# Pooled attention and MLP on one core: a product placed behind the scores, and queries loaded, pooled and bounded in earlier steps

## The chip, the cores and the metric

The kernel runs on one core of a Trainium2 chip. Its engines are TensorE (PE; PEld is its weight load), VectorE (DVE), ScalarE (ACT), GpSimd (POOL) and SyncE (SP), whose queue issues nearly all transfers. The metric is the time of one execution on the device in microseconds (us); less is better.

## The reference, cut to what matters

```python
# q, k, v: (4, 8, 1152, 64); out: (4, 576, 512)
q_pool = q.reshape(B, H, S // 2, 2, D).mean(axis=3)
scores = 1 / sqrt(D) * q_pool @ k.transpose(0, 1, 3, 2)
attn = exp(scores - max(scores)); attn = attn / (sum(attn) + 1e-9)
x = (attn @ v), heads side by side            # (4, 576, 512)
xn = (x - mean(x)) / sqrt(var(x) + 1e-6) * g_ln
out = x + relu(xn @ w_ch1) @ w_ch2            # w_ch1: 512 x 2048, w_ch2: 2048 x 512
```

All of it is in float32.

## The kernel before, in words

**Steps.** Two heads of one batch make a pair; there are 16 pairs (0 to 15), 4 to a batch. A pair is worked off in 9 steps of 128 query rows against 1152 keys (the fifth step takes 64 rows of either head), 144 steps in all. `step(i)` writes the instructions of step i in a fixed order, and each engine works through its own instructions in that order. `on_pe(i)` is true for the first batch, steps 0 to 35. In the list below a pair's steps are counted from its first, and "third step" has index 2.

**What a step does.** TensorE computes the scores of step i+1 (`emit_s`, L365 and L373) into one of two slots of three PSUM banks, by the parity of the step. VectorE takes the row maximum (L384), ScalarE the exponential into a `pe` tile (L398); there are two `pe` buffers, so the exponential of step i overwrites the one of step i-2. In the first batch TensorE transposes the probabilities in float32 (L431), and a product with the values follows (`emit_pv`, L455), its evacuation (L971) and a transposition back (`emit_turn`, L483). From step 36 on the probabilities are split into two float16 parts, the high one by ScalarE (L412), the low one by VectorE (L421) or, in the third, sixth and ninth step of a pair, by GpSimd (L254, then L419; `low_on_pool`). A DMA on the SP queue transposes both (L424), and four steps on the product runs on TensorE (L467). Once a batch is complete, its MLP is spread over later steps in units (L619, L651). These, and transpositions, share PSUM banks 6 and 7, which come free when ScalarE (L632, L289, L580) and VectorE (L633, L286, L581) have read them.

**Queries.** Four loads (`load_q`, L131) bring the queries of an even pair p and of the pair after it, into one of two `qr` buffers. They are pooled by one addition (`pool_q`, L166), then copied to stand twice (`dup_q`, L172), and ScalarE sums their absolute values for the bound on their size (`bound`, L188), which the scale needs (`scales_reduce`, whose VectorE part is L235 to L249). With the scale known, TensorE transposes them (L328) and ScalarE and VectorE split them (L289, L286). Keys (L115) and values (L119) have loads of their own for each pair.

**What sets the order.** Two tables: `pre(i, ...)` puts work ahead of step i's, `at(i, ...)` behind it; and `calm`, a list from which each step takes one piece, in order, mostly of splitting the weights (`w_split_a`, `w_split_b`, `w_split_c`, GpSimd). A loop over the pairs fills the tables; there `i0 = (p - 1) * C` with C = 9 is the first step of the pair before p. For p = 8, 10, 12 and 14 queries are loaded at i0-8, pooled ahead of i0-5 (the fifth step of pair p-2), bounded at i0-3 and copied at i0-1.

Of the kernel before, what the change touches and what calls it, by code (L numbers as in the profile page):

```python
# [14 lines left out]
ALU = mybir.AluOpType  # L15
# [9 lines left out]
def tile_pooled_attention_moe(  # L25
# [18 lines left out]
    nc = tc.nc  # L44
# [110 lines left out]
    def qt_of(p):  # L155
# [2 lines left out]
            st["qt"] = tr_p.tile([128, 2, 2 * C * 64], FP16, tag="qt", name="qt")  # L158
        return st["qt"]

    def pool_q(p, eng, halves=None):

        a = raws[p, "q"]
        for o, n in ((0, 128),) if halves is None else halves:
            x = a[o:o + n].rearrange("p h c r d -> p (h c) r d")
            eng.tensor_tensor(x[:, :, 0], x[:, :, 0], x[:, :, 1], op=ALU.add)  # L166

    def dup_q(p, eng, halves=None):
        a = raws[p, "q"]
        for o, n in ((0, 128),) if halves is None else halves:  # L170
            x = a[o:o + n].rearrange("p h c r d -> p (h c) r d")
            eng.tensor_copy(x[:, :, 1], x[:, :, 0])  # L172

    def bound(p, which, o=0, n=128, junk=None):
        st = state(p)
        if which == "q":
            src = raws[p, "q"][o:o + n].rearrange("p h c r d -> p (h c) r d")[:, :, 0]
            if on_pe((p - 1) * C) or p == 0:
                junk = qt_of(p)[o:o + n, 0].rearrange("p (a d) -> p a d", d=D)
            else:  # L180
                junk = raws[p, "q"][o:o + n].rearrange("p h c r d -> p (h c) r d")[:, :, 1]
        else:
            src = raws[p, which][o:o + n, :, 0:C].rearrange("p a b d -> p a (b d)")
            if junk is None:
                junk = kt_of(p)[o:o + n].rearrange("p a h n -> p (a h n)")[:, 0:S]
                junk = junk.rearrange("p (a n) -> p a n", a=2)
        m = "kqv".index(which)
        nc.scalar.activation(out=junk, in_=src, func=ACTF.Abs, accum_out=st["acc"][o:o + n, m:m + 1])  # L188
# [150 lines left out]
    def on_pe(i):  # L339

        return 0 <= i < HP * C
# [135 lines left out]
    def emit_turn(n, ot, i):  # L477

        j = n % C
        ps = psum[:, 3 * (i % 2) + 2, 128:258]  # L480
        parts = [(h, 64 * h, 64) for h in range(2)] if j == 4 else [(0, 0, 128)]
        for h, q0, w in parts:
            nc.tensor.transpose(ps[0:w, 65 * h:65 * h + 65], ot[:, q0:q0 + w], ident[0:65, 0:65])  # L483
        one, two = evac_pv(n, ps)
        found.extend((one, two, lambda: evacuated(n)))
# [308 lines left out]

    def w_split_c(n):
        x = wsl[:, n + 1].rearrange("p a n -> p (a n)").bitcast(FP32)
        nc.gpsimd.tensor_tensor(wsl[:, n, 1], x, wsl[:, n, 0], op=ALU.subtract)
        w_done[n // 4] += 1


# [2 lines left out]
    def at(i, fn, *a):  # L803
        todo.setdefault(i, []).append((fn, a))
# [10 lines left out]
    for p in range(1, NP):  # L815
# [2 lines left out]
        at(i0, load, p, "v", nc.sync)  # L818
        at(i0 + 1, bound, p, "k")
        if p % 2 == 0:  # L820
            if on_pe(i0):
                at(i0 - 4, load_q, p, (nc.sync,))
                at(i0 - 1, lambda p=p: calm.appendleft((lambda n: pool_q(p, nc.gpsimd), 0)))
                at(i0, lambda p=p: calm.appendleft((lambda n: dup_q(p, nc.gpsimd), 0)))
            else:
                x = i0 - (6 if p == 6 else 5)
                at(i0 - 8, load_q, p, (nc.sync,))
                pre(x, pool_q, p, nc.gpsimd)
                at(i0 - 1, dup_q, p, nc.gpsimd)
            at(i0 + 2 if on_pe(i0) else x + 2, bound, p, "q")  # L830
        elif p == 1:
            upper = (64, 64)
            pre(0, behind_scales)
# [146 lines left out]
    def step(i):  # L980
# [8 lines left out]
            steps.pop(i - 1)  # L989
        while found:  # L990
            found.popleft()()
        first = on_pe(i - 2) or on_pe(i)
        final, last[:] = list(last), []
        if first and not on_pe(i):
            a_piece(i)
# [150 lines left out]
```

## Time and profile before

| | |
|---|---|
| time, median of 3 runs | 839.42 us (837.78 to 840.08) |
| the profiled execution's own time | 839.62 us |
| its span, first to last instruction | 837.8 us |
| TensorE busy | 809.8 us, 97% |
| VectorE busy | 606.2 us, 72% |
| ScalarE busy | 558.4 us, 67% |
| GpSimd busy | 351.8 us, 42% |
| mean granted TensorE clock | 0.993 of full speed |
| moved by DMA | 115.97 MB, mean 138 GB/s |

The span is of one execution, which lies 1.8 us below that execution's time. Busy time is a union of an engine's instructions; TensorE's ends are modelled, so its share reads high.

### The profile page before, as it was taken

To read this page: it belongs to the slowest core of one execution; us is meant where nothing else is said; L and a number is where in the kernel's file an instruction comes from. 1 tells how busy PE (TensorE), PEld (TensorE's weight loads), DVE (VectorE), ACT (ScalarE), POOL (GpSimd) and SP (SyncE) were. 2 spreads that over 40 slices of the span, in tenths; PEclk is the share of its full clock that TensorE was granted. 3 is DMA by queue.
4 is the path that set the end of the run, shared out by engine and by line. 5 is a ranking of instruction groups with operands and counts; after the bars stand their busy time and mean duration, and the time that the engine had idled before them with its cause. 6 is when DMAs were issued, how large, how long until landed. Compare 5 with 4: busy or idle time off the path is not lost.

```text
span 837.8 us, 21673 instructions
## 1 busy us (share of the span) xinstructions
PE 809.8 (97%) x9142; PEld 576.7 (69%) x9142; DVE 606.2 (72%) x1167; ACT 558.4 (67%) x810; POOL 351.8 (42%) x343
## 2 busy tenths in 40 slices
PE   7999999987999989999999999999999999999997
PEld 6787878776666666757576766766666767767764
DVE  3598989887888878797887878888787877522221
ACT  3999898976777868787776777677867676311110
POOL 3020334286899982456452553636343432200000
PEclk9999999999999999999999999999999999999999
DMA  6944474125698998899989988996969866401001
GB/s 146 256 164 156 141 210 163 43 60 113 115 181 141 194 172 191 153 185 185 167 147 166 212 167 144 176 196 113 204 125 194 137 126 131 95 2 26 14 1 25
DMA packets 276018, 115.97 MB, mean 138 GB/s; under 512 B 259280, under 2 KB 259280, under 8 KB 275920
## 3 DMA queue, kind: packets, MB, share of 16 engines
q1 hardware_dynamic: 275568, 113.70, 66.0%
q8 instruction: 71, 1.16, 0.6%
q10 hardware_dynamic: 352, 0.88, 0.5%
q14 instruction: 27, 0.22, 0.1%
HBM read 46.14 MB, written 4.72 MB: 61 GB/s over the span
## 4 chain that ended last, share of the span: by engine, by line
PE 70%; DVE 12%; ACT 9%; DMA 4%; issue 3%; POOL 1%; SPq 1%; ACTq 0%; DVEq 0%; POOLq 0%
PE psum L619 21%; PE psum L651 20%; PE psum L467 10%; PE psum L365 8%; ACT pe L398 3%; DVE mx L384 3%; PE psum L373 2%; PE psum L455 2%; DMA kr<-in_k_dram 2%; PE psum L328 2%; PE psum L431 1%; DVE hl L421 1%; ACT pt L437 1%; PE psum L300 1%; DMA stage<-in_moe_w_ch_dram 1%
## 5 line engine op out<-in xcount | busy, mean ns | idle before, releaser
L384 DVE TENSOR_REDUCE mx<-psum 128x1 f32<-128x1152 f32 x144 | 194.3, 1349 | 21.3 <-PE psum L204 6.9
L398 ACT ACTIVATE pe<-psum,nb,sc 128x1152 f32<-128x1152 f32 x144 | 188.6, 1310 | 13.8 <-DVE r L516 5.7
L651 PE MATMUL psum<-wsl,ht 128*128 128x512 f16 x864 | 196.7, 379 | 0.0
L619 PEld LDWEIGHTS <-wsl 128*128 128x128 f16 x1920 | 170.1, 98 | 22.8 <-issue 4.0
L619 PE MATMUL psum<-xn,wsl 128*128 128x256 f16 x1536 | 177.9, 274 | 3.6 <-DVE ht L633 2.8
L651 PEld LDWEIGHTS <-ht 128*128 128x128 f16 x864 | 80.5, 98 | 88.0
L632 ACT ACTIVATE ht<-psum 128x512 f16<-128x512 f32 x72 | 42.9, 596 | 135.4 <-PE psum L619 134.1
L365 PE MATMUL psum<-kt,qt 64*128 64x512 f16 (+1 forms) x960 | 127.4, 380 | 0.7 <-ACT pe L398 0.5
L412 ACT ACTIVATE hl<-pe 128x1152 f16<-128x1152 f32 x108 | 125.6, 1163 | 3.4
L467 PE MATMUL psum<-vt,pt 128*128 128x65 f16 (+1 forms) x3240 | 117.0, 193 | 0.3 <-DMA pt<-hl 0.3
L467 PEld LDWEIGHTS <-pt 128*128 128x128 f16 (+1 forms) x3240 | 108.5, 100 | 3.1 <-DMA pt<-hl 0.4
L421 DVE SCALAR_TENSOR_TENSOR hl<-pe,hl 128x1152 f16<-128x1152 f32 x72 | 109.4, 1519 | 0.0
L633 DVE SCALAR_TENSOR_TENSOR ht<-psum,ht 128x512 f16<-128x512 f32 x72 | 49.6, 689 | 71.6 <-ACT ht L632 71.6
L254 POOL TENSOR_SCALAR pe<-pe 128x1152 f32<-128x1152 f32 x36 | 42.4, 1178 | 140.5 <-ACT hl L412 140.5
L419 POOL TENSOR_TENSOR hl<-pe,hl 128x1152 f16<-128x1152 f32 x36 | 85.5, 2376 | 3.0
L455 PE MATMUL psum<-pt,vt 128*65 128x128 f32 (+1 forms) x720 | 78.9, 265 | 1.9 <-DVE qt L286 1.9
L455 PEld LDWEIGHTS psum<-pt,vt 128*65 128x65 f32 x720 | 73.1, 140 | 2.2 <-DVE qt L286 2.2
L365 PEld LDWEIGHTS <-qt 64*128 64x128 f16 (+1 forms) x960 | 39.6, 96 | 38.7 <-issue 22.1
L373 PEld LDWEIGHTS <-qt 128*128 128x128 f16 (+1 forms) x320 | 17.2, 99 | 62.9 <-issue 62.7
L286 DVE SCALAR_TENSOR_TENSOR qt<-psum,s,qt 128x384 f16<-128x384 f32 x48 | 29.5, 615 | 34.6 <-ACT qt L289 34.3
L260 POOL COPY gate<-gate 128x1 f32<-128x1 f32 x27 | 5.2, 194 | 110.9 <-DVE gate L259 110.9
L665 DVE SCALAR_TENSOR_TENSOR xb<-psum,inv,xb 128x512 f32<-128x512 f32 x32 | 23.8, 745 | 36.9 <-PE psum L651 36.9
(117 smaller groups left out, 1028.4 us busy)
## 6 DMA issues: line engine op xcount, KB each, us to landing
stage<-in_moe_w_ch_dram SPq DMA_DIRECT2D x32, 512.0 KB, 6.0
kr<-in_k_dram SPq DMA_DIRECT2D x16, 576.0 KB, 4.4
qr<-in_q_dram SPq DMA_DIRECT2D x31, 288.0 KB, 6.2
vr<-in_v_dram SPq DMA_DIRECT2D x15, 576.0 KB, 4.8
out_dram<-xb SPq DMA_DIRECT2D x32, 128.0 KB, 2.4
pt<-hl SPq DMA_TRANSPOSE x108, 4.7
kr<-in_k_dram SPq DMA_DIRECT2D x16, 64.0 KB, 4.1
vr<-in_v_dram ACTq DMA_DIRECT2D x1, 576.0 KB, 7.2
```

Source lines behind the costliest of these rows:

```text
L365: nc.tensor.matmul(out=sp[o:o + w, c0:c0 + 512], lhsT=qt[r:r + 64, qa, q0:q0 + w], rhs=kt[r:r + 64, ka, h], start=(a == 0), stop=(a == 2),)
L384: nc.vector.tensor_reduce(mx, st["s"], axis=AX.X, op=ALU.max)
L398: nc.scalar.activation(out=st["pe"], in_=st["s"], func=ACTF.Exp, scale=pair[i // C]["sc"][:, 0:1], bias=st["nb"],)
L412: nc.scalar.activation(out=hl[:, 0], in_=st["pe"], func=ACTF.Copy, scale=2.0 ** 15)
L419: nc.gpsimd.tensor_tensor(hl[:, 1], st["pe"], hl[:, 0], op=ALU.subtract)
L421: nc.vector.scalar_tensor_tensor(hl[:, 1], st["pe"], 2.0 ** 15, hl[:, 0], op0=ALU.mult, op1=ALU.subtract)
L455: nc.tensor.matmul(out=ps[0:65, q0:q0 + w], lhsT=vt[:, h, c], rhs=pt[:, 128 * u + q0:128 * u + q0 + w], start=(u == 0), stop=(u == C - 1),)
L467: nc.tensor.matmul(out=dst[:, 0:n], lhsT=lhsT, rhs=rhs, start=(u == 0 and lhsT is hi and n == 65), stop=(u == C - 1 and lhsT is lo), skip_ ...
L619: nc.tensor.matmul(out=ps[:, o:o + n], lhsT=wsl[:, 8 * w + cc, wa, f * 128:f * 128 + 128], rhs=xn[:, xa * KD + cc, 0:n], start=(m == 0), s ...
L632: lambda: nc.scalar.activation(out=hi, in_=pv, func=ACTF.Relu),
L633: lambda: nc.vector.scalar_tensor_tensor(lo, pv, 0.0, hi, op0=ALU.max, op1=ALU.subtract),
L651: nc.tensor.matmul(out=ps, lhsT=hv[0][:, ha, f, t * 128:t * 128 + 128], rhs=wsl[:, 8 * w + 4 + f // 2, wa, (f % 2) * DM:(f % 2) * DM + DM] ...
```

## The change

The product of step 34 (`first` in `step`) is written behind the next scores in place of ahead of them, and `emit_turn` takes the other slot's bank from step 36 on. Queries of pairs 4 and 5 are loaded and pooled six steps earlier than they were, copied four and bounded seven. For p = 8, 10, 12, 14 the loads go from i0-8 to i0-9, the pooling from i0-5 to i0-7 (the third step of pair p-2) and the bound from i0-3 to i0-6; for p = 6 the load goes to i0-9, the pooling stays at i0-6, and the bound goes one step ahead. From step 36 on a pooling, a copy and a `w_split_c` is written as two instructions of half the length (`cuts`).

```diff
+    def cuts(x):
+        return (x,) if on_pe(this[0]) else (x[:, 0:C], x[:, C:2 * C])
+
     def pool_q(p, eng, halves=None):
...
-            eng.tensor_tensor(x[:, :, 0], x[:, :, 0], x[:, :, 1], op=ALU.add)
+            for y in cuts(x):
+                eng.tensor_tensor(y[:, :, 0], y[:, :, 0], y[:, :, 1], op=ALU.add)
 
     def dup_q(p, eng, halves=None):
...
-            eng.tensor_copy(x[:, :, 1], x[:, :, 0])
+            for y in cuts(x):
+                eng.tensor_copy(y[:, :, 1], y[:, :, 0])
 
     def bound(p, which, o=0, n=128, junk=None):
...
-            if on_pe((p - 1) * C) or p == 0:
+            if p < 4:
                 junk = qt_of(p)[o:o + n, 0].rearrange("p (a d) -> p a d", d=D)
...
     def emit_turn(n, ot, i):
 
         j = n % C
-        ps = psum[:, 3 * (i % 2) + 2, 128:258]
+        ps = psum[:, 3 * ((i if on_pe(i) else pv_slot[0]) % 2) + 2, 128:258]
...
     def w_split_c(n):
         x = wsl[:, n + 1].rearrange("p a n -> p (a n)").bitcast(FP32)
-        nc.gpsimd.tensor_tensor(wsl[:, n, 1], x, wsl[:, n, 0], op=ALU.subtract)
+        for y in (slice(0, 1024),) if on_pe(this[0]) else (slice(0, 512), slice(512, 1024)):
+            nc.gpsimd.tensor_tensor(wsl[:, n, 1, y], x[:, y], wsl[:, n, 0, y], op=ALU.subtract)
         w_done[n // 4] += 1
...
         if p % 2 == 0:
-            if on_pe(i0):
+            if p == 4:
+                at(i0 - 10, load_q, p, (nc.sync,))
+                at(i0 - 7, lambda p=p: calm.appendleft((lambda n: pool_q(p, nc.gpsimd), 0)))
+                at(i0 - 4, lambda p=p: calm.appendleft((lambda n: dup_q(p, nc.gpsimd), 0)))
+            elif on_pe(i0):
                 at(i0 - 4, load_q, p, (nc.sync,))
                 at(i0 - 1, lambda p=p: calm.appendleft((lambda n: pool_q(p, nc.gpsimd), 0)))
                 at(i0, lambda p=p: calm.appendleft((lambda n: dup_q(p, nc.gpsimd), 0)))
             else:
-                x = i0 - (6 if p == 6 else 5)
-                at(i0 - 8, load_q, p, (nc.sync,))
+                x = i0 - (6 if p == 6 else 7)
+                at(i0 - 9, load_q, p, (nc.sync,))
                 pre(x, pool_q, p, nc.gpsimd)
                 at(i0 - 1, dup_q, p, nc.gpsimd)
-            at(i0 + 2 if on_pe(i0) else x + 2, bound, p, "q")
+            if on_pe(i0):
+                x = i0 + 1 if p == 2 else i0 - 6
+            at(x + 1, bound, p, "q")
...
-        first = on_pe(i - 2) or on_pe(i)
+        first = on_pe(i - 1) or on_pe(i)
```

**On TensorE, steps 37 and 38.** The rows below are of the kernel before: L328 transposes queries, L574 a normalised tile, L455 is the product of step 34, L365 the scores of step 38, L483 the transposition back, L215 spreads a weight bound to all partitions.

```order
L328 MATMUL psum<-ident,qr 128x64 x6
L574 MATMUL psum<-ident,xs 128x128 x4
L455 MATMUL psum<-pt,vt 65x128 x9
L365 LDWEIGHTS qt
L365 MATMUL psum<-kt,qt 128x512
...
L483 MATMUL psum<-ident,pt 128x65
L215 MATMUL psum<-dg,ones_85 128x1
```

The same place in the changed kernel, whose lines are numbered 5 higher there.

```order
L333 MATMUL psum<-ident,qr 128x64 x6
L579 MATMUL psum<-ident,xs 128x128 x4
L370 LDWEIGHTS qt
L370 MATMUL psum<-kt,qt 128x512
...
L460 MATMUL psum<-pt,vt 65x128 x9
L220 MATMUL psum<-dg,ones_85 128x1
```

The product has moved behind the scores of step 38, and the transposition back, which needs it, behind those of step 39.

**On GpSimd, for pair 10 (steps 73 to 76).** Before: L191 copies a bound, L254 and L419 make the low half of the third step's probabilities, L562 to L568 normalise a tile, L166 pools.

```order
L191 COPY acc<-acc 128x1
L254 TENSOR_SCALAR pe<-pe 128x1152
L419 TENSOR_TENSOR hl<-pe,hl 128x1152
L562 TENSOR_SCALAR rs<-mv 128x1
L565 TENSOR_SCALAR rs<-mv 128x1
L566 TENSOR_TENSOR rs<-rs,nhalf 128x1
L568 TENSOR_SCALAR xs<-xb,rs 128x512
L166 TENSOR_TENSOR qr<-qr 128x18x64
```

In the changed kernel.

```order
L196 COPY acc<-acc 128x1
L170 TENSOR_TENSOR qr<-qr 128x9x64 x2
L259 TENSOR_SCALAR pe<-pe 128x1152
L424 TENSOR_TENSOR hl<-pe,hl 128x1152
L567 TENSOR_SCALAR rs<-mv 128x1
L570 TENSOR_SCALAR rs<-mv 128x1
L571 TENSOR_TENSOR rs<-rs,nhalf 128x1
L573 TENSOR_SCALAR xs<-xb,rs 128x512
```

The pooling, now in two halves, stands ahead of the low half and of the normalisation. For pair 8 a piece of splitting (L797, two halves) and a scaling (L254) of weights come between the pooling and the low half; before, the pooling stood behind all of them.

**On the SP queue, for pair 10 (steps 71 to 73).** Before: keys (L115, L116), a transposition of probabilities (L424), values (L119), a transposition, queries (L131).

```order
L115 DMA kr<-in_k_dram 128x2x576
L116 DMA kr<-in_k_dram 128x2x64
L424 DMA_TRANSPOSE pt<-hl 128x18x128
L119 DMA vr<-in_v_dram 128x2x576
L424 DMA_TRANSPOSE pt<-hl 128x18x128
L131 DMA qr<-in_q_dram 64x1152 x4
L670 DMA out_dram<-xb 64x512 x2
```

In the changed kernel.

```order
L115 DMA kr<-in_k_dram 128x2x576
L116 DMA kr<-in_k_dram 128x2x64
L429 DMA_TRANSPOSE pt<-hl 128x18x128
L119 DMA vr<-in_v_dram 128x2x576
L131 DMA qr<-in_q_dram 64x1152 x4
L429 DMA_TRANSPOSE pt<-hl 128x18x128
L675 DMA out_dram<-xb 64x512 x2
```

The four query loads have moved past one transposition, to directly behind the values.

## Rows read from the trace of the kernel before

**Rows 1.** The page: busy us (share of the span) and instructions by engine.

```profile
PE 809.8 (97%) x9142; PEld 576.7 (69%) x9142; DVE 606.2 (72%) x1167; ACT 558.4 (67%) x810; POOL 351.8 (42%) x343
```

**Rows 2.** Timeline, TensorE at the batch boundary: start, us, instructions [idle before <-releaser].

```profile
191.16 3.70 PE L455 MATMUL psum<-pt,vt 128*65 128x128 f32 x18 [1.94 <-DVE qt L286]
```

**Rows 3.** Windows: stretch, us, busy us by engine (instructions), PEclk, DMA share, GB/s.

```profile
190.91:194.32 3.41, 3.16 (x15) 3.16 (x16) 3.26 (x5) 0.00 (x0) 1.28 (x2) 0.50 0.02 5
```

**Rows 4.** Timeline, VectorE at the batch boundary.

```profile
194.02 0.18 DVE L557 BATCH_NORM_AGGREGATE mv<-bs 128x2 f32<-128x6 f32 x1
197.14 1.36 DVE L384 TENSOR_REDUCE mx<-psum 128x1 f32<-128x1152 f32 x1 [2.94 <-PE psum L215]
```

**Rows 5.** Timeline, SP queue: values ahead of pairs 8 to 14's queries; pair 10's.

```profile
285.01 0.58 SPq L119 DMA_DIRECT2D vr<-in_v_dram  x1
...
370.84 0.58 SPq L119 DMA_DIRECT2D vr<-in_v_dram  x1
...
375.83 2.50 SPq L131 DMA_DIRECT2D qr<-in_q_dram  x4
...
457.88 0.58 SPq L119 DMA_DIRECT2D vr<-in_v_dram  x1
...
546.07 0.58 SPq L119 DMA_DIRECT2D vr<-in_v_dram  x1
```

**Rows 6.** By source: landing of all L119; L131 of pair 10, ns, and its landing.

```profile
DMA to landing us min/median/max: 4.4/4.8/7.2
...
L131 SPq DMA_DIRECT2D qr<-in_q_dram x4: 589/592/596, 375.8 to 377.7; - x4
...
DMA to landing us min/median/max: 4.1/5.7/6.7
```

**Rows 7.** Timeline, GpSimd, steps 75 to 77.

```profile
375.92 1.16 POOL L254 TENSOR_SCALAR pe<-pe 128x1152 f32<-128x1152 f32 x1 [6.82 <-ACT hl L412]
377.16 2.38 POOL L419 TENSOR_TENSOR hl<-pe,hl 128x1152 f16<-128x1152 f32 x1
...
384.58 2.62 POOL L166 TENSOR_TENSOR qr<-qr 128x1152 f32<-128x1152 f32 x1 [3.10 <-DMA qr<-in_q_dram]
```

**Rows 8.** By source, L188: bounds of queries in the first batch, ns min/median/max, first and last.

```profile
L188 ACT ACTIVATE qt<-qr x4: 1154/1158/1164, 8.7 to 152.1; 64x1152 f16<-64x1152 f32 x2, 128x1152 f16<-128x1152 f32 x2
```

**Rows 9.** Timeline, TensorE, step 79.

```profile
396.82 0.63 PE L574 MATMUL psum<-ident,xs 128*128 128x128 f32 x4 [0.77 <-DVE qt L286]
```

**Rows 10.** Timeline, GpSimd: a scaling and a split of weights, steps 55 to 59.

```profile
282.25 1.12 POOL L254 TENSOR_SCALAR wsl<-wsl,wscl 128x1024 f32<-128x1024 f32 x1
...
300.56 2.12 POOL L797 TENSOR_TENSOR wsl<-wsl 128x1024 f16<-128x1024 f32 x1
```

**Rows 11.** Timeline, ScalarE: the exponentials of steps 58, 76, 94 and 112.

```profile
295.08 1.31 ACT L398 ACTIVATE pe<-psum,nb,sc 128x1152 f32<-128x1152 f32 x1
...
380.75 1.31 ACT L398 ACTIVATE pe<-psum,nb,sc 128x1152 f32<-128x1152 f32 x1
...
471.23 1.31 ACT L398 ACTIVATE pe<-psum,nb,sc 128x1152 f32<-128x1152 f32 x1
...
559.66 1.31 ACT L398 ACTIVATE pe<-psum,nb,sc 128x1152 f32<-128x1152 f32 x1
```

**Rows 12.** Timeline, VectorE: step 77's evacuation; step 112's low half.

```profile
384.20 0.75 DVE L286 SCALAR_TENSOR_TENSOR kt<-psum,s,kt 128x512 f16<-128x512 f32 x1 [0.43 <-ACT kt L289]
...
560.41 3.60 DVE L421 SCALAR_TENSOR_TENSOR hl<-pe,hl 128x1152 f16<-128x1152 f32 x1
```

**Rows 13.** Timeline, TensorE: pieces behind the exponentials of rows 11.

```profile
303.74 4.34 PE L619 MATMUL psum<-xn,wsl 128*128 128x256 f16 x24 [2.14 <-DVE ht L633]
...
385.36 0.60 PE L574 MATMUL psum<-ident,xs 128*128 128x128 f32 x4
...
477.59 2.75 PE L651 MATMUL psum<-wsl,ht 128*128 128x512 f16 x12
...
566.26 0.63 PE L574 MATMUL psum<-ident,xs 128*128 128x128 f32 x4 [1.77 <-DVE kt L286]
```

## The prediction

> **What bounds the kernel now.** I read the page first, then TensorE's and VectorE's timeline around the batch boundary, then for each even pair the SP queue, GpSimd, ScalarE and TensorE in the stretch where the change puts the pooling. TensorE is busy for 97% of the span [rows 1]. It works in program order, so whatever makes it wait is added to the time, and little is made up for later. At the batch boundary it waits 1.94 us in front of a product (L455), which then takes 3.70 us [rows 2], because the granted clock is 0.50, that is 1.2 GHz, from 190.91 to 194.32 [rows 3]. VectorE meanwhile is through at 194.20 and waits 2.94 us for the next scores [rows 4].
>
> The reader should see a second thing: queries arrive late. For pair 10 the SP queue issues the values at 370.84 and the four query loads from 375.83 [rows 5]; the first load lands 4.1 us after its issue, at 379.9, and the last, issued at 377.7, 6.7 us after, at 384.4 [rows 6]. Three of the four thus take 4.5 us, 1.5 each, and all four about 6.0 us of the DMA engines. GpSimd, now pooling in the fifth step, still waits 3.10 us for them and starts at 384.58 [rows 7].
>
> **The change, part by part.**
>
> *The product behind the scores, its transposition in the other slot.* TensorE has the scores ready to run when the last query transpositions are through, in the gap in which it now waits. The next row maximum can start when VectorE is free, at 194.20 in place of 197.14 [rows 4]: I take -2.9 us, since from there on the same chain follows. Bounds: 0, if the product, still in front of the following scores, holds these up as much; and -3.6, the wait of 1.94 and the 1.7 us that the half clock takes from 3.41 us [rows 2, 3].
>
> *Pair 4's queries earlier, the bound by seven steps.* Its bound leaves ScalarE's queue in step 29 and goes to step 22: 1.16 us [rows 8]. It can be worth all of it where it leaves and cost all of it where it goes, so I take -0.5 between +1.2 and -1.2. GpSimd does the same pieces in another order, and the four loads go out ahead of stage loads in place of among them; both have some steps to spare before anyone reads them: nothing.
>
> *Bounds of the later pairs three steps earlier.* For pair 10 this activation stands in front of the last query evacuations, and TensorE then waits 0.77 us on one [rows 9]: -0.8 (bounds 0 and -0.8; the other pairs show no wait there).
>
> *Pooling in the third step.* Here the DMAs decide. The loads move one step ahead, to directly behind the values, and so in front of one transposition; the pooling moves two steps ahead. The values land 4.8 us (median) after issue [rows 6]; the queries follow them in the queue and need 6.0 us more, so they land 10.8 us after the values' issue. The issues are 285.01, 370.84, 457.88 and 546.07 [rows 5], so they land at 295.8, 381.6, 468.7 and 556.9 for pairs 8, 10, 12 and 14: only about 2.8 us earlier than now for pair 10, while GpSimd comes to them about 9 us earlier. The first half waits for two loads and can begin before the last lands; of a 2.62 us pooling [rows 7] I let 1.6 follow the last landing: 297.4, 383.2, 470.3, 558.5.
>
> GpSimd's queue is in order, and behind the pooling now stands the low half of the third step's probabilities: L254 and L419, 3.6 us from 375.92 to 379.54 [rows 7]. For pair 8 a split in two halves (2.2 us, one whole is 2.12) and a scaling (1.1) [rows 10] stand between. L419 then ends at 304.3, 386.8, 473.9 and 562.1. Who waits: the exponential two steps on, since there are two `pe` buffers. It starts now at 295.08, 380.75, 471.23 and 559.66 [rows 11], so it comes 9.2, 6.1, 2.7 and 2.4 us late.
>
> Behind it ScalarE's queue holds the copy, the output and the evacuation that gives a PSUM bank back. For pair 10 that is 380.75 to the end of VectorE's L286 at 384.95, 4.2 us [rows 11, 12]; where L632 and L633 end it, about 4.0. TensorE's next piece, with two banks, starts at 308.3, 391.0, 477.9 and 566.3 against 303.74, 385.36, 477.59 and 566.26 [rows 13]: +4.6, +5.6, +0.3, 0. In pairs 8 and 14 the present waits (2.14 and 1.77) are thereby paid for and replaced, in pair 8 with the slow clock (4.34 us) as it is. Pair 10 gets a wait over 2 us that it lacks now; one more stretch of 3.41 us at half clock costs 1.7, and I take 1.6. Sum: +12.1. Cutting an instruction in two costs GpSimd a start each, under 0.1 us by the 2.2 above; in these stretches it waits for data longer than that: nothing.
>
> Rate against page: the row says 1.5 us for a load of 0.29 MB, some 197 GB/s. The Trainium skill, SBUF — State Buffer, section "A bandwidth-pool intuition that's wrong", gives HBM to a core about 358 GB/s. An estimate by that page is 3.3 us for all four loads, and a sum near 838; this case's rows don't show such a rate for queries.
>
> *Pair 6* loads one step earlier and pools where it did; its wait was hidden behind the boundary: nothing.
>
> **The sum**, against the profiled execution's 839.6 us: 839.6 - 2.9 - 0.5 - 0.8 + 12.1 = 847.5. The median shown is 839.4, 0.2 below, so 847.3.
>
> **Rivals.**
>
> *The loads are there in time (faster).* If the queries landed before GpSimd has its third-step work, 2.6 us before 375.92 in pair 10, i.e. by 373.3, the pooling would lie in idle time (6.82 us before that instruction [rows 7]), and its halves would hold VectorE less: L421 takes 3.60 us beside the whole pooling in pair 14 [rows 12]. Pair 8 would give back 2.14 + 1.7 and pair 14 1.77: 839.4 - 4.2 - 5.6 = 829.6. On why VectorE is held: the Trainium skill, SBUF — State Buffer, section "Who interferes with whom", has VectorE and GpSimd take a shared port pair for a whole instruction, which this row agrees with. Against this rival: even at the quickest landing, 4.1 us after the last issue, pair 10's queries come at some 377.5. I give 0.17, with what lies between.
>
> *Half as late (no change).* With that quickest landing in all pairs, some 6.6 us behind the values' issue, the poolings end at 293.2, 379.0, 466.1 and 554.3. By the same chain pairs 8 and 10 lose 0.4 and 1.4, pair 12 nothing, and pair 14 gains 1.8: about 835.2, the lower end. At some 8 us behind the issue, a third of the way from that to my 10.8, the four pairs cost a third of 12.1, some 4 us, which is what the earlier parts give: 839.4. For it speaks that the next transposition no longer stands ahead; against it, the engines' 1.5 us for each load. 0.12.
>
> *The boundary gives nothing and the clock falls oftener (much slower).* The loads 0.6 later (6.7 - 4.1 lies over the pure transfer, and the transposition displaced behind them lands late too, so its product waits in step four), 2.4 us; two more slow stretches, 3.2; no gain at the boundary, 2.9: some 856. For it speaks that TensorE's waits in pairs 8 and 10 come in two pieces each; against it, that these waits overlap. 0.16.
>
> *The forecast*, 842 to 852: 0.55.
>
> **How the numbers follow.** A measurement of this kernel tells about 0.3% from no change, 2.5 us. The forecast and the last rival are slower, 0.71; no change 0.12; faster 0.17. The predicted time is the likeliest case, 847. The range reaches down to the quickest landing, 835, and up to 856, leaving out most of the first rival and a little above; the forecast's own is 842 to 852.
>
> **What would show it.** In the changed kernel's trace: before the first half of L166 (now L170) GpSimd waits several us for the query loads in pairs 8 to 14, longest in pair 10; the exponential two steps on waits for GpSimd's L419 by some 9, 6, 2 and 2 us; TensorE has waits there and a granted clock of 0.50 after them. At the boundary VectorE's 2.94 us are gone and there is no slow stretch at 191. Wrong would be a query landing under 8 us after the values' issue, or an exponential that doesn't wait though L419 is late. If the pooling's waits are there and the time isn't longer, TensorE had other room than I saw.

## The result and the profile after

The changed kernel takes **846.12 us** (median of 6 runs, 843.87 to 848.66) against 838.84 (median of 6 runs, 837.52 to 842.41) beside it: a ratio of 1.0076, 95% interval 1.0052 to 1.0100. It is slower by some 7 us. The prediction was 847.0, between 835 and 856, with 0.71 on slower. The size is right. The way to it is right only in part, as the experiments show.

The profiled execution has a span of 845.0 us. First the page of the changed kernel: the engines (answering to [rows 1]), then two of its costliest groups, whose last column is the engine's idle time before them and what ended most of it.

```profile
PE 812.2 (96%) x9142; PEld 577.9 (68%) x9142; DVE 602.8 (71%) x1167; ACT 558.1 (66%) x810; POOL 360.4 (43%) x363
...
L403 ACT ACTIVATE pe<-psum,nb,sc 128x1152 f32<-128x1152 f32 x144 | 188.5, 1309 | 30.9 <-POOL hl L424 18.4
...
L472 PE MATMUL psum<-vt,pt 128*128 128x65 f16 (+1 forms) x3240 | 118.4, 194 | 8.3 <-DMA pt<-hl 8.3
```

TensorE, VectorE and ScalarE have the same instructions as before; GpSimd has 20 more, since some are halved, and is busy 8.6 us longer. What is new is waiting: ScalarE's exponential for GpSimd's low half (L424), 18.4 us in all (3.0 before), its bound for GpSimd's pooling, 9.4 us (none before), and TensorE's product (L472) for a transposition of probabilities by DMA, 8.3 us (0.3 before). The last was only a side remark in one of my rivals.

**Where the time went, step by step.** A step is taken to begin with its row maximum on VectorE (L384 before, L389 after). The table gives how much later that row starts than before, in one profiled execution of each, counted from step 20, up to which the kernels run alike (the starts of step 20 lie within 1.9 us of before's). Pair 4's edit acts up to step 31, the boundary up to 47, and pairs 8, 10, 12 and 14 in the stretches that end at steps 72, 90, 108 and 126. Behind 126 nothing differs.

| us later than before, at step | 31 | 40 | 47 | 56 | 72 | 90 | 108 | 126 |
|---|---|---|---|---|---|---|---|---|
| the change | -1.8 | -8.0 | -6.1 | -6.0 | -1.1 | +3.6 | +4.1 | +7.5 |
| loads four steps earlier | -1.8 | -8.0 | -6.1 | -5.6 | -8.6 | -7.7 | -7.6 | -9.8 |
| pooling back in the fifth step | -1.8 | -8.0 | -6.1 | -5.6 | -8.2 | -8.5 | -8.5 | -9.7 |
| loads of the third step, pooling in the fifth | -1.8 | -7.9 | -6.1 | -5.5 | -2.9 | +1.1 | +1.2 | +0.5 |
| low half on VectorE, bound later | -1.8 | -8.0 | -6.1 | -5.9 | -3.8 | +1.7 | +2.3 | +1.5 |
| loads behind the transposition | -1.8 | -8.0 | -6.1 | -6.0 | +4.3 | +12.2 | +17.8 | +22.6 |
| pooling in the third step alone | 0.0 | 0.0 | -0.1 | -0.1 | +4.6 | +9.6 | +11.3 | +15.7 |
| boundary alone | 0.0 | -5.4 | -0.3 | -0.2 | -2.4 | -1.2 | -1.2 | -1.2 |
| boundary and pair 6's lead | 0.0 | -5.5 | -4.1 | -4.1 | -2.3 | -2.6 | -2.6 | -1.2 |

So the change gains 6 us by step 56 and loses 4.9, 4.7, 0.5 and 3.4 us in pairs 8, 10, 12 and 14.

At the boundary, TensorE's and then VectorE's timeline of the changed kernel answer to [rows 2, 4], and the first window below to [rows 3].

```profile
187.87 2.18 PE L460 MATMUL psum<-pt,vt 128*65 128x128 f32 x18 [0.97 <-DVE qt L291]
...
191.63 2.13 PE L460 MATMUL psum<-pt,vt 128*65 128x128 f32 x18
```

```profile
190.65 0.18 DVE L562 BATCH_NORM_AGGREGATE mv<-bs 128x2 f32<-128x6 f32 x1
190.75 1.32 DVE L389 TENSOR_REDUCE mx<-psum 128x1 f32<-128x1152 f32 x1
```

The product of step 34 (187.87) stands behind the scores and waits 0.97 us in place of 1.94, the row maximum of step 38 follows VectorE's last instruction at once in place of 2.94 us later, and there is no half clock. The windows of the changed kernel (stretch, us, busy us by engine, PEclk, DMA share, GB/s) show where it is now:

```profile
190.91:194.32 3.41, 3.41 (x33) 2.89 (x30) 3.31 (x9) 2.65 (x5) 3.04 (x8) 1.00 1.10 173
292.53:299.36 6.83, 6.03 (x48) 4.80 (x49) 5.93 (x6) 0.79 (x3) 6.75 (x5) 0.50 0.41 92
384.69:388.10 3.41, 3.41 (x17) 2.61 (x18) 2.62 (x8) 2.77 (x4) 3.13 (x5) 0.50 0.87 164
572.42:575.83 3.41, 3.41 (x37) 2.06 (x37) 3.38 (x6) 3.15 (x4) 0.00 (x0) 0.50 0.71 133
```

The granted clock is 0.50 (1.2 GHz) in pairs 8, 10 and 14, in pair 8 from within a TensorE wait of 3.54 us on, in pairs 10 and 14 from 1.3 and 0.6 us behind the end of waits of 3.41 and 2.44 us (rows further down).

Pair 10 shows the loss best. Its SP queue, answering to [rows 5], has the queries directly behind the values, and one transposition behind them:

```profile
369.90 0.58 SPq L119 DMA_DIRECT2D vr<-in_v_dram  x1
370.53 2.44 SPq L131 DMA_DIRECT2D qr<-in_q_dram  x4
373.12 6.67 SPq L429 DMA_TRANSPOSE pt<-hl  x1
```

By source, the four query loads of pair 10 (as [rows 6]): first and last issue, and us to their landing.

```profile
L131 SPq DMA_DIRECT2D qr<-in_q_dram x4: 527/592/595, 370.5 to 372.4; - x4
...
DMA to landing us min/median/max: 5.6/6.7/7.6
```

The last lands at 372.4 + 7.6 = 380.0, 10.1 us behind the values' issue; I had forecast 10.8. GpSimd in pairs 10 and 14 (as [rows 7]):

```profile
378.94 2.75 POOL L170 TENSOR_TENSOR qr<-qr 128x576 f32<-128x576 f32 x2 [11.56 <-DMA qr<-in_q_dram]
381.66 1.15 POOL L259 TENSOR_SCALAR pe<-pe 128x1152 f32<-128x1152 f32 x1
382.89 2.37 POOL L424 TENSOR_TENSOR hl<-pe,hl 128x1152 f16<-128x1152 f32 x1
...
560.14 1.40 POOL L170 TENSOR_TENSOR qr<-qr 128x576 f32<-128x576 f32 x1 [11.88 <-DMA qr<-in_q_dram]
562.60 1.40 POOL L170 TENSOR_TENSOR qr<-qr 128x576 f32<-128x576 f32 x1 [1.06 <-DMA qr<-in_q_dram]
```

ScalarE, the bound (L193) and the exponential (L403, as [rows 11]) in pairs 8, 10, 12 and 14:

```profile
291.58 1.16 ACT L193 ACTIVATE qr<-qr 128x1152 f32<-128x1152 f32 x1 [2.72 <-POOL qr L170]
...
299.57 1.32 ACT L403 ACTIVATE pe<-psum,nb,sc 128x1152 f32<-128x1152 f32 x1 [6.25 <-POOL hl L424]
...
381.72 1.16 ACT L193 ACTIVATE qr<-qr 128x1152 f32<-128x1152 f32 x1 [3.18 <-POOL qr L170]
...
385.29 1.31 ACT L403 ACTIVATE pe<-psum,nb,sc 128x1152 f32<-128x1152 f32 x1 [1.83 <-POOL hl L424]
...
472.54 1.16 ACT L193 ACTIVATE qr<-qr 128x1152 f32<-128x1152 f32 x1 [0.29 <-POOL qr L170]
...
476.12 1.31 ACT L403 ACTIVATE pe<-psum,nb,sc 128x1152 f32<-128x1152 f32 x1 [1.81 <-POOL hl L424]
...
564.03 1.16 ACT L193 ACTIVATE qr<-qr 128x1152 f32<-128x1152 f32 x1 [3.23 <-POOL qr L170]
...
567.61 1.31 ACT L403 ACTIVATE pe<-psum,nb,sc 128x1152 f32<-128x1152 f32 x1 [1.84 <-POOL hl L424]
```

GpSimd holds ScalarE for 9.0, 5.0, 2.1 and 5.1 us in the four pairs (the two waits added). But TensorE's timeline, answering to [rows 9, 13], names another releaser for its two longest waits:

```profile
293.33 1.65 PE L472 MATMUL psum<-vt,pt 128*128 128x65 f16 x27 [3.54 <-DMA pt<-hl]
...
383.36 0.99 PE L472 MATMUL psum<-vt,pt 128*128 128x65 f16 x27 [3.41 <-DMA pt<-hl]
...
564.57 0.99 PE L472 MATMUL psum<-vt,pt 128*128 128x65 f16 x27 [0.94 <-DMA pt<-hl]
...
571.83 0.63 PE L579 MATMUL psum<-ident,xs 128*128 128x128 f32 x4 [2.44 <-DVE kt L291]
```

The transposition that now stands behind the queries, issued at 373.12, ends TensorE's wait at 383.36, 10.2 us later.

A wait need not be what the end of the run hangs on. The chain of work that ended last, followed back from the last instruction, passes these two transpositions by. In pair 8 it is this (start, us, what):

```profile
281.36 7.30 DMA qr<-in_q_dram
...
297.17 2.38 POOL hl L424
...
299.57 1.33 ACT pe L403
...
302.81 0.70 DVE ht L638
...
303.55 2.78 PE psum L624 x24
```

In pairs 10 and 14 it likewise runs from the query loads through GpSimd's low half and the exponential; in pair 12 alone of the four it runs through a transposition (465.34 to 474.98). GpSimd's queue, the prediction's path, thus ends last in the three pairs that lose most, and the displaced transposition lies beside it.

### The profile page after: what moved, and what is told of

Same layout as the page of the kernel before. It is cut to its first block, busy times and chain, and to the rows that moved or that the text cites. A ratio compares the mean times of both kernels' runs of the same rounds, so it can differ in the third digit from the quotient of the medians.

```text
span 845.0 us, 21685 instructions
## 1 busy us (share of the span) xinstructions
PE 812.2 (96%) x9142; PEld 577.9 (68%) x9142; DVE 602.8 (71%) x1167; ACT 558.1 (66%) x810; POOL 360.4 (43%) x363
## 4 chain that ended last, share of the span: by engine, by line
PE 57%; POOL 14%; DVE 9%; ACT 8%; DMA 6%; issue 3%; SPq 1%; POOLq 0%; ACTq 0%; DVEq 0%
PE psum L656 18%; PE psum L624 16%; PE psum L472 8%; PE psum L370 7%; ACT pe L403 3%; POOL hl L424 3%; DMA qr<-in_q_dram 3%; DVE mx L389 3%; POOL wsl L259 3%; POOL wsl L803 2%; PE psum L378 2%; POOL pe L259 1%; PE psum L333 1%; PE psum L460 1%; PE psum L436 1%
## 5 line engine op out<-in xcount | busy, mean ns | idle before, releaser
L403 ACT ACTIVATE pe<-psum,nb,sc 128x1152 f32<-128x1152 f32 x144 | 188.5, 1309 | 30.9 <-POOL hl L424 18.4
L389 DVE TENSOR_REDUCE mx<-psum 128x1 f32<-128x1152 f32 x144 | 194.3, 1349 | 16.3 <-PE psum L472 6.6
L472 PE MATMUL psum<-vt,pt 128*128 128x65 f16 (+1 forms) x3240 | 118.4, 194 | 8.3 <-DMA pt<-hl 8.3
L637 ACT ACTIVATE ht<-psum 128x512 f16<-128x512 f32 x72 | 42.8, 595 | 125.0 <-PE psum L624 124.7
L472 PEld LDWEIGHTS <-pt 128*128 128x128 f16 (+1 forms) x3240 | 109.8, 101 | 11.6 <-DMA pt<-hl 9.0
L424 POOL TENSOR_TENSOR hl<-pe,hl 128x1152 f16<-128x1152 f32 x36 | 86.5, 2403 | 3.0
```

The lines of the kernel that those rows point to most:

```text
L389: nc.vector.tensor_reduce(mx, st["s"], axis=AX.X, op=ALU.max)
L403: nc.scalar.activation(out=st["pe"], in_=st["s"], func=ACTF.Exp, scale=pair[i // C]["sc"][:, 0:1], bias=st["nb"],)
L424: nc.gpsimd.tensor_tensor(hl[:, 1], st["pe"], hl[:, 0], op=ALU.subtract)
L472: nc.tensor.matmul(out=dst[:, 0:n], lhsT=lhsT, rhs=rhs, start=(u == 0 and lhsT is hi and n == 65), stop=(u == C - 1 and lhsT is lo), skip_ ...
```

## The experiments

**Theory one** is the prediction's: the queries land some 10 us behind the values, GpSimd's queue waits for them, and what stands behind the pooling there is late. **Theory two** grew out of TensorE's waits in the trace after: the loads also push back the transposition behind them, and the product waits for that. The rival to both is that the pooling's new place costs by itself, whenever the data come.

### Query loads four steps earlier

```diff
-                at(i0 - 9, load_q, p, (nc.sync,))
+                at(i0 - (9 if p == 6 else 13), load_q, p, (nc.sync,))
```

> The change as it stands, with one edit: the query loads of pairs 8, 10, 12 and 14 go out four steps (some 18 us) earlier; the pooling stays in the third step. Theory (GpSimd waits for queries that land 10 to 12.6 us after the values' issue, and everything queued behind the pooling is late): the steps 56 to 61, 76 to 79 and 112 lose their 5.0, 4.7 and 3.4 us again, pair 12 its 0.5: 846.1 - 13.6 = 832.5, no GpSimd gap before L170 that a DMA ends, no half clock at 292, 384 and 572. First rival (it is the place of the pooling and of the bound in the engines' queues, whenever the data come): 844 to 848. Second rival (the loads now push other transpositions back, so that other products wait): 836 to 842, with TensorE waits on the transposed probabilities.

Measured: 828.80 us, ratio to before 0.9883 (0.9862 to 0.9905). On GpSimd's timeline in this run the poolings of pairs 8 and 10 have no wait in front, in the same third step:

```profile
279.28 2.77 POOL L170 TENSOR_TENSOR qr<-qr 128x576 f32<-128x576 f32 x2
...
359.68 3.89 POOL L170 TENSOR_TENSOR qr<-qr 128x576 f32<-128x576 f32 x2
```

With loads this early the place of the pooling costs nothing; the late loads cost all of it, and more than the 13.6 us that I had put back, since pairs 8 and 14 now lose waits that the kernel before has. This run doesn't tell theory one from two, because the loads left both places at once. One expectation missed: in pair 10 the clock fell again, at 367.95, behind TensorE waits of 1.11 and 0.56 us.

### Pooling back in the fifth step

Pairs 8 to 14 as before the change; the rest as changed.

```diff
-                x = i0 - (6 if p == 6 else 7)
-                at(i0 - 9, load_q, p, (nc.sync,))
+                x = i0 - (6 if p == 6 else 5)
+                at(i0 - (9 if p == 6 else 8), load_q, p, (nc.sync,))
...
-            at(x + 1, bound, p, "q")
+            at(x + (2 if p > 6 else 1), bound, p, "q")
```

> The change with its last part undone for pairs 8, 10, 12 and 14: loads in the second step, pooling in the fifth, bound two steps behind it, as before the change; boundary, pair 4, pair 6 and the halved instructions as changed. Theory: what is left is the gain up to step 56 of the changed kernel's trace, 6.7 us less 0.6 at the very start, on 838.8: about 832.7. Rival (the boundary's gain is given back later whatever the pooling does, or the halved instructions cost something in each pair): 836 to 840.

Measured: 831.42 us, 0.9923 (0.9897 to 0.9948). The other parts together are a gain of 6 to 8 us, as the trace after said.

### Pooling in the third step alone

The kernel before with only that part.

```diff
-                x = i0 - (6 if p == 6 else 5)
-                at(i0 - 8, load_q, p, (nc.sync,))
+                x = i0 - (6 if p == 6 else 7)
+                at(i0 - (8 if p == 6 else 9), load_q, p, (nc.sync,))
...
-            at(i0 + 2 if on_pe(i0) else x + 2, bound, p, "q")
+            at(i0 + 2 if on_pe(i0) else x + (2 if p == 6 else 1), bound, p, "q")
```

> The kernel before with one part of the change: for pairs 8, 10, 12 and 14 loads a step earlier, pooling in the third step, bound behind it; everything else as before. Theory: the loss of the four pairs alone, 5.0 + 4.7 + 0.5 + 3.4 = 13.6 on 838.8: 852.4. My prediction's terms would have it 12.1 - 0.8 more than before: 850.1. Rival (the loss needs the other parts, such as the halved instructions or the shifted steps behind the boundary): 840 to 846.

Measured: 853.68 us, 1.0179 (1.0152 to 1.0205): 15 us lost, 4.6, 5.0, 1.7 and 4.3 in the four pairs by the table. The loss needs none of the other parts. With the run before it the change is made up within the noise: -0.8% and +1.8% are +1.0%, against +0.76% (0.52 to 1.00) measured.

### Low half on VectorE, bound later

The loads stay late; what TensorE needs soon is taken from behind the pooling.

```diff
-        return i % C in (2, 5, 8)
+        return i % C in ((5, 8) if i // C in (6, 8, 10, 12) else (2, 5, 8))
...
-            at(x + 1, bound, p, "q")
+            at(x + (3 if p > 6 else 1), bound, p, "q")
```

> The change with the late loads as they are, but with nothing queued behind the late pooling that TensorE needs soon: the low half of the third step's probabilities in pairs 6, 8, 10 and 12 is made by VectorE in place of GpSimd, and the bound of pairs 8 to 14 stands two steps later in ScalarE's queue. Theory (the loss comes through what is queued behind the pooling: the low half that frees the exponential's buffer, and the bound in front of the next exponential): GpSimd still waits for the loads, as long as now, and the 13.6 us come back but for VectorE's four low halves of 1.3 us and a late split of weights: 832 to 838. Rival (the loads or the pooling cost by themselves, by DMA share or by holding VectorE): 842 or more.

Measured: 840.11 us, 1.0021 (1.0007 to 1.0035). Neither expectation is met: some 6 of the 13.6 us come back. GpSimd still waits (12.28 us in pair 10), now with nothing urgent behind it. TensorE's timeline in this run shows what took over:

```profile
292.10 1.59 PE L472 MATMUL psum<-vt,pt 128*128 128x65 f16 x27 [3.62 <-DMA pt<-hl]
...
380.82 1.57 PE L472 MATMUL psum<-vt,pt 128*128 128x65 f16 x27 [3.77 <-DMA pt<-hl]
```

Theory one alone, as the whole loss, falls here. The two runs below were made to separate it from theory two.

### Loads of the third step, pooling in the fifth

Against the run with the pooling in the fifth step, only the loads' place differs.

```diff
-                at(i0 - (9 if p == 6 else 8), load_q, p, (nc.sync,))
+                at(i0 - 9, load_q, p, (nc.sync,))
```

> The run with the pooling back in the fifth step, with one difference: the query loads of pairs 8 to 14 stay where the change puts them, behind the values and in front of one transposition of probabilities. Theory two (the loads cost by themselves: the transposition queued behind them lands late, and TensorE's product waits for it, 3.5 and 3.4 us in pairs 8 and 10, 0.4 and 0.9 in 12 and 14, with a half clock after a wait or two): 831.4 + 8.2 = 839.6, up to 843 with the clock. Theory one (the loss comes only through GpSimd's queue behind the pooling): 831 to 832.

Measured: 841.15 us, 1.0022 (1.0003 to 1.0041), 9.7 above the 831.42 of the same kernel with the loads behind the transposition. TensorE's timeline, then GpSimd's in pair 10, without a wait, then the chain that ended last, in pair 8:

```profile
292.82 1.65 PE L472 MATMUL psum<-vt,pt 128*128 128x65 f16 x27 [3.64 <-DMA pt<-hl]
...
380.19 1.40 PE L472 MATMUL psum<-vt,pt 128*128 128x65 f16 x27 [2.73 <-DMA pt<-hl]
...
561.77 0.99 PE L472 MATMUL psum<-vt,pt 128*128 128x65 f16 x27 [1.26 <-DMA pt<-hl]
```

```profile
377.70 3.89 POOL L170 TENSOR_TENSOR qr<-qr 128x576 f32<-128x576 f32 x2
```

```profile
282.57 10.21 DMA pt<-hl
```

So the loads cost some 10 us by themselves, with nobody waiting for the queries: here the chain does run through the transposition, in pairs 8 and 10.

### Loads behind the transposition, pooling in the third

The opposite: the transposition goes first, and GpSimd's queue waits longer.

```diff
-                at(i0 - 9, load_q, p, (nc.sync,))
+                at(i0 - (9 if p == 6 else 8), load_q, p, (nc.sync,))
```

> The change with the query loads of pairs 8 to 14 one step later, so behind that transposition, as before the change; the pooling stays in the third step. Theory two alone: the products' waits for the transposition are gone in pairs 8 and 10, 832 to 838. Theory one: the loads land about 4.4 us later than now (384.4 against 380.0 in pair 10), GpSimd's queue and the exponential behind it are late by as much more, and some 3 us come on top in each of three pairs: about 855. If both act side by side, each hiding the other in the changed kernel: slower than the change, 850 or more, with no product waiting for a transposition there and the exponential's wait ended by GpSimd.

Measured: 861.17 us, 1.0259 (1.0229 to 1.0289). ScalarE's and then TensorE's timeline of this run, pairs 8 and 10:

```profile
295.54 1.16 ACT L193 ACTIVATE qr<-qr 128x1152 f32<-128x1152 f32 x1 [6.41 <-POOL qr L170]
...
303.52 1.31 ACT L403 ACTIVATE pe<-psum,nb,sc 128x1152 f32<-128x1152 f32 x1 [6.24 <-POOL hl L424]
...
390.69 1.16 ACT L193 ACTIVATE qr<-qr 128x1152 f32<-128x1152 f32 x1 [6.69 <-POOL qr L170]
```

```profile
298.06 1.12 PE L305 MATMUL psum<-ident,kr 128*128 128x128 f32 x4 [4.16 <-DVE ht L638]
...
304.88 1.46 PE L370 MATMUL psum<-kt,qt 64*128 64x512 f16 x6 [5.71 <-ACT pe L403]
...
393.21 4.22 PE L624 MATMUL psum<-xn,wsl 128*128 128x256 f16 x24 [6.22 <-DVE ht L638]
```

No product waits for a transposition in these two pairs, and from step 56 to 126 this run loses 28.6 us by the table, against 13.5 in the change. Part of the 15 us more is that the loads now land later still (GpSimd waits 14.73 us for them in pair 10, against 11.56), part is clock (a mean of 0.982 granted, against 0.990).

Both theories act. In the change they lie side by side: taking GpSimd's path away and leaving the transposition late gives back 5 to 6 us (the two runs above), taking both away 15 to 17. By the table's columns the loss with the transposition alone, in those two runs, is 2.1 and 2.6 us of 4.9 in pair 8, 5.5 and 4.0 against 4.7 in pair 10, and none in pair 14, where the change loses 3.4. So pair 14 is GpSimd's alone and pair 8 has a share of both; in pair 10 the transposition alone makes the whole loss, though in the change it is GpSimd's path that ends last there. What GpSimd's path would cost by itself with the queries landing as in the change is not shown: this run, which takes the transposition's delay away, also moves the landing.

The rows correct the chain in ScalarE too. In pair 10 it isn't first held by the exponential but by the bound, which the change puts directly behind the pooling in the third step; behind it in the queue stands the evacuation (L637) that gives TensorE its PSUM bank back.

### Boundary alone

The kernel before with only the part at the batch boundary.

```diff
-        ps = psum[:, 3 * (i % 2) + 2, 128:258]
+        ps = psum[:, 3 * ((i if on_pe(i) else pv_slot[0]) % 2) + 2, 128:258]
...
-        first = on_pe(i - 2) or on_pe(i)
+        first = on_pe(i - 1) or on_pe(i)
```

> The kernel before with one part of the change: at the batch boundary the product of step 34 goes behind the scores and its transposition into the other slot; nothing else. My prediction: 2.9 us less, 835.9. By the changed kernel's trace (steps 36 to 40 run 6.2 us faster than before, step 41 gives some of it back behind pair 6's pooling): with pair 6 as before, 6.2 less, 832.6, if the loss in step 41 belongs to pair 6's earlier bound and loads; 835 to 837 if it comes whatever pair 6 does.

Measured: 837.61 us, 0.9989 (0.9970 to 1.0007). Steps 36 to 40 gain 5.4 us and steps 40 to 47 lose 5.1 of them. The SP queue of this run, then GpSimd, then TensorE:

```profile
194.55 2.87 SPq L424 DMA_TRANSPOSE pt<-hl  x1
197.47 2.50 SPq L131 DMA_DIRECT2D qr<-in_q_dram  x4
```

```profile
205.76 2.61 POOL L166 TENSOR_TENSOR qr<-qr 128x1152 f32<-128x1152 f32 x1 [3.00 <-DMA qr<-in_q_dram]
```

```profile
214.45 1.47 PE L365 MATMUL psum<-kt,qt 64*128 64x512 f16 x6 [4.08 <-ACT pe L398]
```

Pair 6's loads stand behind a transposition that the faster boundary doesn't move (193.47 in the kernel before, whose step 20 starts 1.1 us earlier); its queries come too late, and the same chain takes the gain back, with a half clock from 213.09.

### Boundary and pair 6's lead

The run above, with pair 6's loads and bound one step earlier, as in the change.

```diff
-                at(i0 - 8, load_q, p, (nc.sync,))
+                at(i0 - (9 if p == 6 else 8), load_q, p, (nc.sync,))
...
-            at(i0 + 2 if on_pe(i0) else x + 2, bound, p, "q")
+            at(i0 + 2 if on_pe(i0) else x + (1 if p == 6 else 2), bound, p, "q")
```

> The kernel before with two parts of the change: the boundary part and pair 6's (its query loads one step earlier, which puts them in front of the transposition of step 36's probabilities in the SP queue, and its bound one step earlier). Theory (in the run of the boundary part alone the SP queue issues pair 6's loads only at 197.47, behind that transposition, and GpSimd and the exponential of step 40 wait for them, which takes back what the boundary gave; in the changed kernel they are issued at 182.43): the net gain of steps 36 to 47 in the changed kernel, 4.3 us, on 839.1: about 834.8, no half clock near 213. Rival (pair 6's lead is worth nothing, as my prediction had it): 837 to 838, as the boundary alone.

Measured: 834.48 us, 0.9939 (0.9918 to 0.9961), as expected. Its profiled execution was the longest of its runs (838.97), so the table's last column stands above the median; up to step 56 it has the 4.1 us. The SP queue:

```profile
185.05 2.39 SPq L131 DMA_DIRECT2D qr<-in_q_dram  x4
193.69 7.93 SPq L424 DMA_TRANSPOSE pt<-hl  x2
```

One step in the program moved these loads ahead of the transposition, and by 12.4 us (11.6 with the starts of step 20 put together). The bound moved by one step with them; the two weren't separated.

### Boundary alone, pair 6's pooling a step later

Against the run of the boundary alone.

```diff
-                x = i0 - (6 if p == 6 else 5)
+                x = i0 - 5
```

> The kernel before with the boundary part alone, as in the run of that part alone, and pair 6's pooling one step later, so behind the low half of step 38 in GpSimd's queue. Theory (the boundary gives some 5.4 us in steps 36 to 40, and pair 6's queries, which land after the pooling's turn, take it back in step 41 by the same queue): the exponential of step 40 comes 5 to 6 us earlier than in the run of the boundary part alone, no half clock after it, 834 to 835. Rival (step 41 gives it back whatever pair 6 does): 837 to 838, as the boundary alone.

Measured: 837.94 us, 0.9993 (0.9977 to 1.0009): no better than the boundary alone, a miss. The exponential of step 40 does come earlier (204.53 against 213.09, with the start 1.9 us earlier), without a half clock. But VectorE's low half then runs beside the pooling, 3.62 us in place of 1.4 to 1.5, and TensorE waits 2.90 us for an evacuation behind it. The profiled execution (835.74, the quickest of its runs) has kept 3.1 us at step 56; in the median nothing is left. Why the other runs lose it isn't settled.

### Pair 4 alone

The kernel before with the edits for pair 4 (loads, pooling, duplication, bound).

```diff
-            if on_pe((p - 1) * C) or p == 0:
+            if p < 4:
...
-            if on_pe(i0):
+            if p == 4:
+                at(i0 - 10, load_q, p, (nc.sync,))
+                at(i0 - 7, lambda p=p: calm.appendleft((lambda n: pool_q(p, nc.gpsimd), 0)))
+                at(i0 - 4, lambda p=p: calm.appendleft((lambda n: dup_q(p, nc.gpsimd), 0)))
+            elif on_pe(i0):
...
-            at(i0 + 2 if on_pe(i0) else x + 2, bound, p, "q")
+            at((i0 + 2 if p == 2 else i0 - 5) if on_pe(i0) else x + 2, bound, p, "q")
```

> The kernel before with one part of the change: pair 4's queries loaded, pooled and duplicated early and its bound seven steps earlier; nothing else. My prediction: 0.5 us less than before (838.6), between 1.2 less and 1.2 more. By the changed kernel's trace (its steps 21 to 31 run 1.8 us faster than before): 837.3. Rival (that gain is only pushed to the boundary and waits there, since the row maximum of step 38 is late for another reason): 839.

Measured: 837.16 us, 0.9980 (0.9963 to 0.9998). The 1.8 us of the trace are there at step 31, and stay.

### Loads early, nothing halved

The run with the loads four steps earlier, with every halved instruction whole again.

```diff
-        return (x,) if on_pe(this[0]) else (x[:, 0:C], x[:, C:2 * C])
+        return (x,)
...
-        for y in (slice(0, 1024),) if on_pe(this[0]) else (slice(0, 512), slice(512, 1024)):
+        for y in (slice(0, 1024),):
```

> The change with the query loads of pairs 8 to 14 four steps earlier, as in the first run, and all halved instructions whole again (pooling, duplication, weight split). My prediction has the halving at nothing: 828.8 within 1. Rival (a whole pooling of 2.6 us holds VectorE's low halves longer than two of 1.4): 830 to 832. Other rival (each cut costs GpSimd a start that the path feels): 827 or less.

Measured: 829.70 us, 0.9887 (0.9870 to 0.9905), beside 828.80 (0.9862 to 0.9905) with the halves. No difference, within what can be measured; With late loads the halving wasn't tried by itself; the third step alone, with whole instructions, loses some 2 us more in the four pairs than the change, and whether that is the halving's isn't shown.

### Pair 6 early as well

The run with the loads four steps earlier, and pair 6 loaded in step 30 and pooled in step 32. The line with `state` only allocates pair 5's tiles ahead of pair 6's.

```diff
-                x = i0 - (6 if p == 6 else 7)
-                at(i0 - (9 if p == 6 else 13), load_q, p, (nc.sync,))
+                x = i0 - (13 if p == 6 else 7)
+                at(i0 - (15 if p == 6 else 13), load_q, p, (nc.sync,))
...
-            at(x + 1, bound, p, "q")
+            if p == 6:
+                at(x + 1, state, 5)
+            at(x + 1, bound, p, "q")
```

> The first run (query loads of pairs 8 to 14 four steps earlier, 828.8) with pair 6 treated likewise: its loads six steps earlier, in step 30, and its pooling and bound seven steps earlier, in steps 32 and 33, where GpSimd has some 5 us free. Theory (step 41's loss of 2.6 us against the kernel before is GpSimd's full queue with pair 6's pooling in it, in front of the low half that the exponential of step 40 waits for): that step is 2 to 2.6 us shorter, 826 to 827. Rival (the weight splits fill GpSimd's queue there with or without the pooling): 828 to 829.

Measured: 829.18 us, 0.9878 (0.9849 to 0.9906): no gain. Step 41 is 2.6 us shorter, as the theory has it, but step 32, where the pooling now stands, is 1.84 longer. The best version stays the one with the loads four steps earlier, 10.3 us below before and 17.3 below the change.

## Why the prediction came out

**The query landing: right.** 10.4, 10.1, 10.0 and 12.6 us behind the values' issue, against 10.8. By the first and last landing of pair 10, 376.1 and 380.0, a load takes 1.3 us, or 0.29 MB at some 226 GB/s. The Trainium skill, SBUF — State Buffer, section "A bandwidth-pool intuition that's wrong", has some 358 GB/s from HBM to a core; my estimate by it was a sum near 838. The trace doesn't show that rate for these loads, and the measurement decides. GpSimd's wait is longest in pair 12 (13.3 us), not in pair 10 (11.56) as I said.

**ScalarE's lateness: right in size in three pairs, wrong in its first link.** Forecast 9.2, 6.1, 2.7 and 2.4 us late; GpSimd holds ScalarE for 9.0, 5.0, 2.1 and 5.1. I had the exponential wait for its buffer by all of that; its own wait is 6.25, 1.83, 1.81 and 1.84, and in front of it the bound, which I left out of ScalarE's queue, waits for the pooling. In pair 14 the two come to twice the forecast.

**TensorE's wait: the step that failed.** "TensorE's next piece, with two banks, starts at 308.3, 391.0, ..." made the whole loss out of GpSimd's queue. That path does end last in pairs 8, 10 and 14 of the change. But in pairs 8 and 10 TensorE first waits for the displaced transposition (3.54 and 3.41), which by itself costs some 10 us, and with it there GpSimd's path adds only 5 to 6. I priced that displacement at a share of 2.4 us in a rival and at nothing in the sum. The sum held because the two delays overlap, which no term of mine weighed; a second term of 10 us for it would have made the sum too high by about that.

**The terms.** Pair 8: +4.6 forecast, +4.9 in the table. Pair 10 with its clock stretch and bound: +5.6 + 1.6 - 0.8 = +6.4, against +4.7. Pair 12: +0.3, +0.5. Pair 14: 0, against +3.4: mis-sized, as the values themselves landed later there (6.2 us after their issue, not 4.8, and the queries 12.6, not 10.8), and a wait of 2.44 us was followed by a half clock.

**Boundary and pair 6: mis-sized, and not separable.** The boundary was put at -2.9 and pair 6 at nothing. Alone, the boundary gives nothing measurable; with pair 6's lead it gives 4 to 5 us. "Its wait was hidden behind the boundary" was true of the kernel before, but the boundary was the cover, and the change removes it. **Pair 4**: -0.5 within ±1.2, measured -1.8 in the trace, outside these bounds, and -0.2% in time. **Halving**: nothing in time, as forecast, though a halved pooling takes 2.75 us against 2.62 and a halved split 2.27 against 2.12, more than the 0.1 that I allowed.

These misses are opposed, some 2.6 us more gained ahead of pair 8 and some 2 us more lost behind it, and so 847.0 came as close to 846.1 as it did: the direction was reasoned, the last few us were luck.

## What to carry to other kernels

A load that is moved past another transfer in an in-order queue has two prices: when its own data land, and when the transfer that it displaced lands. One can hide the other, so undoing one shows too little. Test them apart and together, and read at each place which of the two the last chain runs through; moving the load back also moves its own landing, so that run doesn't isolate the second price. An earlier consumer needs an earlier load: the same pooling place cost 15 us with late loads and nothing with early ones. And where an edit is costed at nothing because a wait covers it, ask whether another part of the same change takes that wait away.

## What was not expected of the hardware

A transposition by DMA held the SP queue for longer behind loads that were still under way: 6.67 us for the one behind pair 10's queries, where the one at 194.55 in the boundary-alone run held it 2.87, and it landed 10.2 us after its issue. In pairs 8, 10 and 14 its hold ended within 0.2 us of the last query landing (379.79 against 380.0 in pair 10), as if it waited for that; why isn't shown. And moving a load by one step in the program, past one such transposition, moved its issue by 12.4 us (185.05 against 197.47).

The granted clock fell to 0.50 at waits of 2.4 to 3.5 us in the changed kernel, but in the run with early loads behind waits of 1.11 and 0.56 us as well. With the pooling in the fifth step and the loads behind the transposition, the profiled execution, the quickest of its runs, has no half clock at all between the first step and the last. Which kernel loses the 1.7 us of such a stretch could not be read from the lengths of the waits alone.
